# Sparse attention with mixture of experts: constants written in three pieces, and the placings of two batches at other units

## The chip, the core and the metric

The kernel runs on one core of one Trainium2 chip. The time is device time in microseconds (us) of one execution. It was measured three times before the change; a profile of one further execution gives the trace. The engines are PE (TensorE, matmuls), DVE (VectorE), ACT (ScalarE), POOL (GpSimd) and SP (which only issues DMAs here). Each engine works through its own list of instructions strictly in order, and waits at an instruction until all that it needs is there.

## What is computed

Chunk-selected causal attention over 4 batches of 8 heads with 768 positions and 64 columns, then a mixture of experts over the 3072 resulting tokens: a dense two-layer part for every token, and for each token one of 8 experts, chosen by the largest logit and weighted by its softmax value.

```python
# attention: the 6 best chunks of 32 keys by an upper bound, then causal softmax
ub = np.sum(np.maximum(q[:, :, :, None, :] * k_min[:, :, None, :, :], q[:, :, :, None, :] * k_max[:, :, None, :, :]), axis=-1)
top_chunks = np.argsort(ub, axis=-1)[..., -top_k:]
mask = sel & (pos[:, None] >= pos[None, :])
scores = np.where(mask, scores, -1000000000.0)
...
# mixture of experts on x = the attention output, a row per token
y_dense = np.maximum(x @ w1_dense, 0.0) @ w2_dense
expert_idx = np.argmax(x @ w_gate, axis=1)
for e in range(E):
    mask = expert_idx == e
    h = np.maximum(x[mask] @ w1[e], 0.0)
    y_moe[mask] = gate_w[mask, None] * (h @ w2[e])
return (y_dense + y_moe).astype(np.float32)
```

## The kernel before

**The attention** runs over 16 pairs of heads, four pairs to a batch; here pair 0 to pair 15. A pair has 11 units, 0 to 10. A unit computes a tile of up to 128x512 scores on PE (`scores`, L603), takes the exponential on ACT into `ex` (L607), and multiplies it with the values on PE (`av`, L622, into `op`). Scores are issued two units ahead of their `av`. In units 0, 5 and 6 the tile lies on the diagonal, and POOL masks `ex` (the select, L609) between ACT and the `av`. When a head's last `av` is done, DVE normalises it (`norm`, L631 and L633) into `xbig`, the batch's token rows. There are two `xbig`, so batch 2 writes the one that batch 0 used.

**Preparation for later pairs** runs beside this: SP loads k, q and v; POOL casts v of pair p+2 at unit 0 of pair p (L534) and k and q of pair p+3 at unit 7 (L527, L529); PE turns them round (L540, L560, L589); DVE reduces keys to chunk extremes `ks` (L545), multiplies them with a mask into `kb` (L548), copies halves of k (L552, L553), and finds the best chunks by MAX8 (L581) into flags `fl` (L583). PE needs `kb` for the bounds `ub` (L575). POOL also issues the casting loads of the weights: `wd` (L206, L208) and the experts' `we` (L213), one to three in a pair.

**A finished batch** is worked on during the next batch's 44 units, in slots that `batch_fills` keys by number; the slot of key n runs at unit n+1 of the batch. PE turns token rows round (L262), computes the gate (L270), the dense layers (L407, L423) and, at key 15, each token's row number in its expert's list (`ranks`, which ends in `slot` on DVE, L307). Then `place(t)`, for t from 0 to 5, has POOL scatter 128 token rows of `xbig` into `table` by an indirect DMA (L387). `place(0)` is preceded by a small copy of token numbers (L381). The placings stood at keys 18, 21, 24, 27, 30 and 33: units 8 of the batch's second pair, 0, 3, 6 and 9 of its third, and 1 of its fourth.

**The constants** that gate, ranks, placings and lists need are written by `route_consts`, all at once at unit 0 of pair 2, behind the value cast and the second `wd` load. It ends with a DMA on SP of an empty block, `zt`, into `table` (L194).

**The order** on each engine is set when the program is built: a helper schedules instructions by their dependences, and `tc.issue_after` pins an instruction behind another; `latest["pool"]` is the select issued last. The last batch's tail (from about 160 us) runs the experts over fetched rows of `table` and scatters their outputs from POOL.

Of the kernel before, what the change touches and what calls it, by code (L numbers as in the profile page):

```python
# [12 lines left out]
ALU = mybir.AluOpType  # L13
# [4 lines left out]
def kernel(  # L18
# [147 lines left out]
    nblk = const.tile([1, 1], mybir.dt.int32)  # L166
    xbig = [const.tile([128, NT, XW], HF, name=f"xbig{i}") for i in range(2)]

    def route_consts():
        for x2 in xbig:  # L170
            nc.gpsimd.memset(x2[:, :, Dm:XW], 0.0)
        nc.gpsimd.iota(iom8, pattern=[[0, NT], [1, E]], base=-E, channel_multiplier=0, allow_small_or_imprecise_dtypes=True)
        nc.gpsimd.memset(osum[:, 0], 0.0)
        nc.gpsimd.memset(eone, 1.0)
        nc.gpsimd.memset(used, 0.0)
        for i in range(EF):
            nc.gpsimd.memset(we_[:, :, i : i + 1], float(E**i))
        for i in range(RF):
            nc.gpsimd.memset(wr_[:, :, i : i + 1], float(256**i))
        for f in (EF, RF):  # L180
            for t in fields[f]:
                nc.gpsimd.memset(t, 0.0)
        nc.gpsimd.memset(ones, 1.0)
        nc.gpsimd.memset(low, 1.0)
        nc.gpsimd.affine_select(out=low, in_=low, compare_op=ALU.is_gt, fill=0.0,
                                base=0, pattern=[[1, 128]], channel_multiplier=-1)
        nc.gpsimd.iota(ebase[:, 0], pattern=[[CAP // 128, E]], base=0, channel_multiplier=0, allow_small_or_imprecise_dtypes=True)
        nc.gpsimd.iota(erow, pattern=[[CAP, E]], base=0, channel_multiplier=0, allow_small_or_imprecise_dtypes=True)
        nc.gpsimd.iota(iob, pattern=[[1, NBLK]], base=0, channel_multiplier=0, allow_small_or_imprecise_dtypes=True)
        for j in range(NJ):  # L190
            nc.gpsimd.iota(num[64 * j : 64 * j + 64, :, 0], pattern=[[128, NM]], base=j, channel_multiplier=2)
        nc.gpsimd.memset(zt, 0)
        nc.gpsimd.memset(zt[:, Dm + 2 : Dm + 4].bitcast(mybir.dt.int32), NONE)
        nc.sync.dma_start(out=table[EMPTY : EMPTY + 128], in_=zt)  # L194


    wd = const.tile([128, 2 * NK, 512], HF)
# [55 lines left out]
    def batch_fills(b):  # L253
# [197 lines left out]
        for n, f in zip((0, 2, 4, 6, 8, 10) + (12,), out_list):  # L451
            at.setdefault(n, []).append(f)
        at.setdefault(15, []).append(ranks)
        for t in range(NT):
            at.setdefault(18 + 3 * t, []).append(place(t))
        for n, f in zip((7, 8, 9, 10, 12, 13, 14, 15, 17, 18, 19, 20, 22, 23, 24, 25, 27, 28, 29, 30, 32, 33, 34, 35, 37, 38, 39, 40), dense):
            at.setdefault(n, []).append(f)
        return out_list, dense, ranks, [place(t) for t in range(NT)], at
# [56 lines left out]
    with (  # L515
# [234 lines left out]

        wq = [(e, w) for w in range(2) for e in range(E)]
        PER_PAIR = {**{p: 1 for p in range(4, 10)}, 10: 2, 11: 2, 12: 2, 13: 3}
        ahead_n = 2
        LAG = 1

# [11 lines left out]
        for i, (p, u) in enumerate(seq):  # L767
# [43 lines left out]
            if u == (6 if p == 0 else 0) and n2 is not None:  # L811
                with tc.issue_after(latest["pool"].ins):
                    cast_v(n2)
                load(p + 4, "v")
                if 1 <= p <= 2:
                    load_dense(st[n2]["cast"], p - 1)
                if p == 2:
                    with tc.issue_after(st[n2]["cast"].ins):
                        route_consts()
                for _ in range(PER_PAIR.get(p, 0)):  # L820
                    load_expert(*wq.pop(0), st[n2]["cast"])
            if u == 0 and p == NP - 2:
                while wq:
                    load_expert(*wq.pop(0), latest["pool"])
            if u == 7:
                with tc.issue_after(latest["pool"].ins):
                    cast_qk(p + 3)
                load(p + 5, "kq")
# [169 lines left out]
```

## Time and profile before

| | us |
|---|---|
| median of 3 runs (lowest, highest) | 246.07 (245.33, 246.31) |
| the profiled execution, its own time | 247.03 |
| its span in the trace | 245.3 |
| PE busy | 209.9 (86%) |
| DVE busy | 176.5 (72%) |
| ACT busy | 174.4 (71%) |
| POOL busy | 162.3 (66%) |

The span runs from the first to the last recorded instruction; 1.73 us of the profiled execution lie outside it. The share of an engine is an average over stages with different limits, so the stages have to be read one by one: a view by windows gives the busy time of each engine in a stretch, and the timeline of an engine gives its instructions in order of time, with the idle time before each and what ended it. A DMA row gives the time from issue to landing.

### The profile page before, as it was taken

Reading aid. Unit: us, or ns where it says so; the run is one execution under the profiler, and the core shown is the slowest. Engines: PE = TensorE matmul, PEld = TensorE weight load, DVE = VectorE, ACT = ScalarE, POOL = GpSimd, SP = SyncE. Lnnn points to the kernel's source line nnn. Section 1 sums busy time; section 2 is a strip of 40 time slices with the busy share of each in tenths; the row PEclk is TensorE's granted clock in tenths of the full one; section 3 lists DMA queues with packets and bytes.
Section 4 is the critical chain, followed back from the end, with each engine's and each line's share of the span. In section 5 each row is a group of like instructions: output and inputs, shape, how many; then the busy total and the mean of one; then the engine's idle time right before and its main releaser. Section 6 shows DMA issues by size and latency. Waiting matters only on the chain. (4 is left out here: it accounts for less than half of the span.)

```text
span 245.3 us, 7890 instructions
## 1 busy us (share of the span) xinstructions
PE 209.9 (86%) x2771; PEld 149.1 (61%) x2771; DVE 176.5 (72%) x561; ACT 174.4 (71%) x325; POOL 162.3 (66%) x213
## 2 busy tenths in 40 slices
PE   0688778798997989997999997989999989999950
PEld 0466455665665667754668665667566657777720
DVE  3889999999989789796978998677632225555410
ACT  4579797888787899596899986844566556666630
POOL 6458796677188767358878827620788748888881
PEclk9999999999999999999999999999999999999996
DMA  6999999999479899989999999356499999987785
GB/s 176 249 268 277 204 250 223 273 207 240 139 111 351 171 300 243 254 175 208 334 157 263 196 181 229 116 149 180 141 273 226 221 269 245 190 138 106 96 117 99
DMA packets 68279, 50.55 MB, mean 206 GB/s; under 512 B 29712, under 2 KB 61328, under 8 KB 68240
## 3 DMA queue, kind: packets, MB, share of 16 engines
q1 hardware_dynamic: 53008, 30.72, 46.7%
q0 software_dynamic: 15232, 19.32, 46.4%
q8 instruction: 23, 0.38, 0.6%
q14 instruction: 16, 0.13, 0.2%
HBM read 41.93 MB, written 18.23 MB: 245 GB/s over the span
## 5 line engine op out<-in xcount | busy, mean ns | idle before, releaser
L607 ACT ACTIVATE ex<-sp 128x512 f16<-128x512 f32 (+1 forms) x176 | 91.6, 606 | 10.3 <-PE sp L603 8.5
L603 PE MATMUL sp<-rT,kT 128*128 128x128 f16 (+3 forms) x384 | 64.2, 261 | 3.6 <-ACT ex L607 0.9
L609 POOL TENSOR_SCALAR_AFFINE_SELECT ex<-ex 128x512 f16<-128x512 f16 x48 | 32.5, 687 | 37.9 <-ACT ex L607 35.6
L897 POOL DMA_INDIRECT out_dram<-yo,xg x27 | 44.8, 1658 | 12.1 <-issue 4.9
L622 PE MATMUL op<-v,ex 128*128 128x65 f16 x672 | 46.0, 194 | 7.3 <-POOL ex L609 4.2
L622 PEld LDWEIGHTS <-ex 128*128 128x128 f16 x672 | 36.1, 98 | 23.1 <-POOL ex L609 8.1
L387 POOL DMA_INDIRECT table<-xbig,slot x24 | 24.4, 1015 | 17.8 <-issue 17.2
L860 DVE COPY exT<-tp 128x512 f16<-128x512 f16 x28 | 11.8, 423 | 33.1 <-PE tp L858 28.7
L603 PEld LDWEIGHTS <-kT 128*128 128x128 f16 x384 | 28.4, 98 | 7.5 <-issue 4.6
L867 PEld LDWEIGHTS <-w 128*128 128x128 f16 x432 | 26.4, 98 | 8.1 <-issue 2.4
L888 PE MATMUL yp<-we,ehT 128*128 x112 | 30.8, 378 | 0.5 <-ACT ys L428 0.2
L867 PE MATMUL hp<-exT,w 128*128 128x128 f16 x432 | 29.2, 219 | 0.8 <-issue 0.8
L407 PE MATMUL hp<-xT,wd 128*128 128x384 f16 x128 | 28.9, 325 | 0.6 <-DVE xT L263 0.6
L895 ACT ACTIVATE yo<-yp,xg 128x512 f32<-128x512 f32 x27 | 18.6, 687 | 14.0 <-PE yp L888 13.2
L545 DVE TENSOR_REDUCE ks<-kp 128x24 f16<-128x768 f16 x28 | 25.4, 946 | 3.6 <-ACT kp L542 3.3
L423 PE MATMUL yp<-wd,hT 128*128 128x512 f16 x96 | 25.9, 379 | 0.3
L870 ACT ACTIVATE ehT<-hp 128x512 f16<-128x512 f32 x28 | 16.7, 597 | 12.4 <-PE hp L867 9.1
L412 ACT ACTIVATE hT<-hp 128x384 f16<-128x384 f32 x30 | 14.9, 498 | 10.7 <-PE hp L407 10.1
L512 DVE COPY w<-we 128x2048 f16 x27 | 18.7, 694 | 0.2 <-DVE exT L860 0.2
L633 DVE TENSOR_TENSOR xbig<-op,rs 128x384 f16<-128x384 f32 x32 | 17.6, 550 | 0.3
L428 ACT COPY ys<-yp 128x512 f32<-128x512 f32 x21 | 12.7, 606 | 6.0 <-PE yp L423 5.9
L888 PEld LDWEIGHTS <-ehT 128*128 128x128 f16 x112 | 10.1, 97 | 10.2 <-issue 3.6
(158 smaller groups left out, 371.6 us busy)
## 6 DMA issues: line engine op xcount, KB each, us to landing
we<-in_moe_w_dram POOLq DMA_DIRECT2D x16, 512.0 KB, 7.6
kf<-in_k_dram SPq DMA_DIRECT2D x32, 192.0 KB, 4.0
qf<-in_q_dram SPq DMA_DIRECT2D x32, 192.0 KB, 4.5
vf<-in_v_dram SPq DMA_DIRECT2D x32, 192.0 KB, 4.8
out_dram<-ys SPq DMA_DIRECT2D x48, 128.0 KB, 5.3
xg<-table SPq DMA_DIRECT2D x27, 136.0 KB, 4.1
table<-zt SPq DMA_DIRECT2D x9, 136.0 KB, 2.4
wd<-in_moe_w_dense_dram POOLq DMA_DIRECT2D x2, 512.0 KB
```

The source lines that it names most:

```text
L387: sc = nc.gpsimd.indirect_dma_start(out=table, out_offset=bass.IndirectOffsetOnAxis(ap=keep["slot"][:, t : t + 1], axis=0), in_=xbig[b % 2 ...
L407: nc.tensor.matmul(hp, wd[:, ko, j * 128 : (j + 1) * 128], xT[:, ko, g * G * 128 : (g + 1) * G * 128], start=(ko == 0), stop=(ko == NK - 1))
L423: nc.tensor.matmul(yp, hold["h"][:, j, i * 128 : (i + 1) * 128], wd[:, NK + j], start=(j == 0), stop=(j == NK - 1))
L512: nc.vector.tensor_copy(w.rearrange("p j f -> p (j f)"), w1f[:, bass.ds(offs1[i], NK * 512)])
L545: nc.vector.tensor_reduce(out=ks[:, i], in_=kp.rearrange("d (c w) -> d c w", w=32), op=op, axis=mybir.AxisListType.X)
L603: last = nc.tensor.matmul(sp[:, o : o + w], kT[p % NB][g][:, kt * 128 : (kt + 1) * 128], rT[p % NB][g][:, a * 128 : z * 128], start=(o == ...
L607: scored.append((last, nc.scalar.activation(ex[:, 0:o], sp[:, 0:o], AF.Exp, scale=-0.125)))
L609: latest["pool"] = nc.gpsimd.affine_select(out=ex, in_=ex, compare_op=ALU.is_ge, fill=0.0, base=0, pattern=[[0, 4], [1, 2], [2, 64]], chan ...
L622: nc.tensor.matmul(s["op", g][:, t * (D + 1) : (t + 1) * (D + 1)], ex[:, o : o + 128], v16[p % NB][:, g, kt, :], start=first, stop=(last_o ...
L867: nc.tensor.matmul(hp[:, j], s["w1"][:, ko, j * 128 : (j + 1) * 128], s["xT"][:, ko], start=(ko == 0), stop=(ko == NK - 1), skip_group_che ...
L888: nc.tensor.matmul(yp, s["hT"][:, j], w2f[:, bass.ds(offs[i] + j * 512, 512)], start=(j == 0), stop=(j == NK - 1))
L897: sc = nc.gpsimd.indirect_dma_start(out=out, out_offset=to, in_=o, in_offset=None, bounds_check=N - 1, oob_is_err=False, compute_op=ALU.by ...
```

## The change

`route_consts` takes a part number. Part 0 holds the tails of both `xbig`, `iom8`, the first `osum`, `ones` and `low`; part 1 `ebase`, `num`, the empty block `zt` and its DMA; part 2 all the small ones of the lists (`eone`, `used`, the weights, the fields, `erow`, `iob`). They are issued at unit 5 of pairs 3, 4 and 5, behind the select issued last (that of unit 6), where all stood at unit 0 of pair 2. For batches 0 and 1 the placings move to keys 25, 26, 31, 36, 37 and 42: units 4, 5 and 10 of the batch's third pair and the same of its fourth. Batch 2 keeps its keys.

```diff
-    def route_consts():
+    def route_consts(part):
+        if part == 0:
             for x2 in xbig:
                 nc.gpsimd.memset(x2[:, :, Dm:XW], 0.0)
...
+        elif part == 1:
...
-        for t in range(NT):
-            at.setdefault(18 + 3 * t, []).append(place(t))
+        for t, n in enumerate((25, 26, 31, 36, 37, 42) if b < B - 2 else range(18, 36, 3)):
+            at.setdefault(n, []).append(place(t))
...
+        CONSTS = (3, 4, 5)
...
-                if p == 2:
-                    with tc.issue_after(st[n2]["cast"].ins):
-                        route_consts()
...
+            if u == 5 and p in CONSTS:
+                with tc.issue_after(latest["pool"].ins):
+                    route_consts(CONSTS.index(p))
```

On POOL in pair 2, before: the value cast, the load of `wd`, the constants (30 instructions, cut here), then the selects of units 5 and 6 and the cast of k.

```order
L534 CAST v_1_119<-vf 128x12x64
L208 DMA wd<-in_moe_w_dense_dram 128x4x512
L171 MEMSET xbig_171 128x6x32
...
L193 MEMSET zt 128x1
L609 AFFINE_SELECT ex<-ex 128x512 x2
L527 CAST k_902<-kf 128x768
```

The same place after, and on to pair 3 (lines are numbered three higher from `route_consts` on):

```order
L537 CAST v_1_119<-vf 128x12x64
L211 DMA wd<-in_moe_w_dense_dram 128x4x512
L612 AFFINE_SELECT ex<-ex 128x512 x2
L530 CAST k_871<-kf 128x768
L532 CAST q_873<-qf 128x768
L612 AFFINE_SELECT ex<-ex 128x512
L537 CAST v_2_120<-vf 128x12x64
L612 AFFINE_SELECT ex<-ex 128x512 x2
L172 MEMSET xbig_171 128x6x32
...
L176 MEMSET low 128x128
L530 CAST k_1069<-kf 128x768
```

The selects of pair 2 now follow the load of `wd` at once, and a first piece of the constants stands between the selects of pair 3 and its cast of k.

On POOL in pairs 6 and 7, before, batch 0's placings stand round the selects of units 5 and 6 of pair 6, and ahead of the value cast of pair 7:

```order
L387 DMA table<-xbig_171,slot 25728x544 x2
L609 AFFINE_SELECT ex<-ex 128x512
L387 DMA table<-xbig_171,slot 25728x544
L609 AFFINE_SELECT ex<-ex 128x512
L387 DMA table<-xbig_171,slot 25728x544
L527 CAST k_1832<-kf 128x768
L529 CAST q_1834<-qf 128x768
L609 AFFINE_SELECT ex<-ex 128x512
L387 DMA table<-xbig_171,slot 25728x544 x2
L534 CAST v_0_118<-vf 128x12x64
L213 DMA we_175<-in_moe_w_dram 128x4x512
L609 AFFINE_SELECT ex<-ex 128x512 x2
```

After, from the selects of pair 7's units 5 and 6 into pair 8, whose unit 0 select is the first single one:

```order
L612 AFFINE_SELECT ex<-ex 128x512 x2
L390 DMA table<-xbig_171,slot 25728x544 x2
L530 CAST k_2058<-kf 128x768
L532 CAST q_2060<-qf 128x768
L612 AFFINE_SELECT ex<-ex 128x512
L390 DMA table<-xbig_171,slot 25728x544
L537 CAST v_1_119<-vf 128x12x64
L216 DMA we_175<-in_moe_w_dram 128x4x512
L612 AFFINE_SELECT ex<-ex 128x512 x2
```

The fourth and fifth placing now stand behind pair 7's selects, and the sixth in pair 8, ahead of its value cast, its expert load and its selects of units 5 and 6. In pair 6 the first two stand between the casts of k and of q, behind both selects; batch 1 has the same pattern in pairs 10, 11 and 12.

On DVE in pair 8, the normalisation that first writes batch 2's rows into batch 0's `xbig`, with the semaphores that it waits for; six of them are those of batch 0's placings, before and after:

```order
L631 RECIPROCAL rs<-op 128x6 [waits PE_49]
L633 TENSOR_TENSOR xbig_171<-op,rs 128x6x64 [waits DMASW3_49,DMASW2_49,DMASW6_49,DMASW1_49,DMASW7_49,DMASW0_49,DVE_49]
L545 TENSOR_REDUCE ks<-kp 128x24 [waits Activation_49]
...
L564 TENSOR_SCALAR rT_0_114<-pq 128x768 [waits Activation_49]
L548 TENSOR_TENSOR kb<-ks,hmask 128x96 [waits DVE_49]
```

```order
L634 RECIPROCAL rs<-op 128x6 [waits PE_49]
L636 TENSOR_TENSOR xbig_171<-op,rs 128x6x64 [waits DMASW4_49,DMASW3_49,DMASW6_49,DMASW2_49,DMASW7_49,DMASW0_49,DVE_49]
L548 TENSOR_REDUCE ks<-kp 128x24 [waits Activation_49]
...
L567 TENSOR_SCALAR rT_0_114<-pq 128x768 [waits Activation_49]
L551 TENSOR_TENSOR kb<-ks,hmask 128x96 [waits DVE_49]
```

Its place on DVE has not moved, while the last of the placings that it waits for has moved from pair 7 to pair 8.

## Rows read from the trace of the kernel before

**Rows 1.** The view by windows of 20 us over all engines: start and end, length, then busy time and number of instructions of PE, its weight loads, DVE, ACT and POOL, the granted PE clock as a share of 2.4 GHz, the DMA share and GB/s.

```profile
20.00:40.00 20.00, 15.95 (x251) 11.27 (x249) 19.43 (x54) 16.83 (x33) 16.88 (x50) 1.00 1.15 241
...
100.00:120.00 20.00, 17.93 (x261) 12.62 (x257) 16.61 (x58) 15.68 (x33) 11.84 (x16) 1.00 1.03 235
```

**Rows 2.** POOL's timeline in pair 2, at and behind the constants: start, busy us, what, and the idle time before it with what ended it.

```profile
32.78 0.48 POOL L171 MEMSET xbig<- 128x192 f16 x2
...
33.41 0.17 POOL L174 MEMSET eone<- 1x8 f32 x1
...
34.00 0.19 POOL L183 MEMSET ones<- 128x128 f16 x1
...
34.29 0.13 POOL L187 IOTA ebase<- 128x8 f16 x1
34.38 0.13 POOL L188 IOTA erow<- 1x8 f32 x1
...
34.60 0.36 POOL L191 IOTA num<- 64x24 int32 x2
...
35.52 0.29 POOL L185 TENSOR_SCALAR_AFFINE_SELECT low<-low 128x128 f16<-128x128 f16 x1
...
35.82 1.27 POOL L609 TENSOR_SCALAR_AFFINE_SELECT ex<-ex 128x512 f16<-128x512 f16 x2
...
37.81 0.82 POOL L529 CAST q<-qf 128x768 f16<-128x768 f32 x1
```

**Rows 3.** ACT's timeline in pair 2: the six exponentials of units 4 to 9.

```profile
32.59 3.03 ACT L607 ACTIVATE ex<-sp 128x384 f16<-128x384 f32 x6
```

**Rows 4.** DVE's timeline in pairs 1 to 3; the reductions L545 come once in a pair.

```profile
27.06 1.80 DVE L545 TENSOR_REDUCE ks<-kp 128x24 f16<-128x768 f16 x2
...
32.80 0.68 DVE L553 COPY kT<-kp 64x768 f16<-64x768 f16 x1
...
35.39 1.80 DVE L545 TENSOR_REDUCE ks<-kp 128x24 f16<-128x768 f16 x2
...
37.81 0.88 DVE L548 TENSOR_TENSOR kb<-ks,hmask 128x96 f16<-128x96 f16 x1
...
43.81 1.80 DVE L545 TENSOR_REDUCE ks<-kp 128x24 f16<-128x768 f16 x2
...
46.23 0.21 DVE L548 TENSOR_TENSOR kb<-ks,hmask 128x96 f16<-128x96 f16 x1
```

**Rows 5.** PE's timeline: the two waits in pair 2, the wait in pair 6, two products of pair 8 (units 5 and 6), the wait in pair 10 and the products of unit 5 in pair 12.

```profile
36.53 0.30 PE L622 MATMUL op<-v,ex 128*128 128x65 f16 x4 [0.62 <-POOL ex L609]
37.15 0.30 PE L622 MATMUL op<-v,ex 128*128 128x65 f16 x4 [0.32 <-POOL ex L609]
...
77.84 0.21 PE L575 MATMUL ub<-kb,qp 128*128 128x48 f16 x2 [1.25 <-DVE kb L548]
...
91.14 0.30 PE L622 MATMUL op<-v,ex 128*128 128x65 f16 x4
...
112.69 0.30 PE L622 MATMUL op<-v,ex 128*128 128x65 f16 x4 [1.62 <-POOL ex L609]
...
132.82 0.32 PE L622 MATMUL op<-v,ex 128*128 128x65 f16 x5
```

**Rows 6.** POOL's timeline in pairs 6 to 8: the cast and the select about `kb` in pair 6, the select of pair 7's unit 6, and the start of pair 8.

```profile
76.28 0.83 POOL L529 CAST q<-qf 128x768 f16<-128x768 f32 x1
77.05 0.67 POOL L609 TENSOR_SCALAR_AFFINE_SELECT ex<-ex 128x512 f16<-128x512 f16 x1
...
83.27 0.67 POOL L609 TENSOR_SCALAR_AFFINE_SELECT ex<-ex 128x512 f16<-128x512 f16 x1 [0.84 <-ACT ex L607]
...
88.00 0.74 POOL L609 TENSOR_SCALAR_AFFINE_SELECT ex<-ex 128x512 f16<-128x512 f16 x1 [2.53 <-ACT ex L607]
...
90.42 1.28 POOL L609 TENSOR_SCALAR_AFFINE_SELECT ex<-ex 128x512 f16<-128x512 f16 x2 [0.17 <-ACT ex L607]
```

**Rows 7.** DVE's timeline: `kb` in pair 6, a key copy and the first normalisation of pair 8, and a key copy in pair 11.

```profile
76.39 1.40 DVE L548 TENSOR_TENSOR kb<-ks,hmask 128x96 f16<-128x96 f16 x1
...
87.05 0.31 DVE L552 COPY kT<-kp 64x768 f16<-64x768 f16 x1
...
92.60 0.56 DVE L633 TENSOR_TENSOR xbig<-op,rs 128x384 f16<-128x384 f32 x1
...
118.79 0.36 DVE L553 COPY kT<-kp 64x768 f16<-64x768 f16 x1
```

**Rows 8.** POOL's timeline in pairs 10 to 12: batch 1's placings, and the selects of pair 12's units 5 and 6.

```profile
109.60 1.04 POOL L387 DMA_INDIRECT table<-xbig,slot  x1 [1.64 <-issue]
110.94 1.01 POOL L387 DMA_INDIRECT table<-xbig,slot  x1 [0.31 <-issue]
111.96 0.67 POOL L609 TENSOR_SCALAR_AFFINE_SELECT ex<-ex 128x512 f16<-128x512 f16 x1
...
118.73 0.98 POOL L387 DMA_INDIRECT table<-xbig,slot  x1 [0.17 <-issue]
...
130.99 1.30 POOL L609 TENSOR_SCALAR_AFFINE_SELECT ex<-ex 128x512 f16<-128x512 f16 x2
```

**Rows 9.** The DMA view of two windows of some 1 us, each with one placing: its queue, the number of issues, and the us from issue to landing. The first is batch 0's first placing, the second batch 1's fifth.

```profile
table<-xbig,slot POOLq DMA_INDIRECT x1, 6.5
...
table<-xbig,slot POOLq DMA_INDIRECT x1, 5.1
```

More of the change, by code (lines that the diff above doesn't have):

```diff
@@ L167 @@
     xbig = [const.tile([128, NT, XW], HF, name=f"xbig{i}") for i in range(2)]
-    def route_consts():
[L170 to L194, printed above, removed]
@@ new lines, in route_consts @@
+    def route_consts(part):
+        if part == 0:
+            for x2 in xbig:
+                nc.gpsimd.memset(x2[:, :, Dm:XW], 0.0)
+            nc.gpsimd.iota(iom8, pattern=[[0, NT], [1, E]], base=-E, channel_multiplier=0, allow_small_or_imprecise_dtypes=True)
+            nc.gpsimd.memset(osum[:, 0], 0.0)
+            nc.gpsimd.memset(ones, 1.0)
+            nc.gpsimd.memset(low, 1.0)
+            nc.gpsimd.affine_select(out=low, in_=low, compare_op=ALU.is_gt, fill=0.0,
+                                    base=0, pattern=[[1, 128]], channel_multiplier=-1)
+        elif part == 1:
+            nc.gpsimd.iota(ebase[:, 0], pattern=[[CAP // 128, E]], base=0, channel_multiplier=0, allow_small_or_imprecise_dtypes=True)
+            for j in range(NJ):
+                nc.gpsimd.iota(num[64 * j : 64 * j + 64, :, 0], pattern=[[128, NM]], base=j, channel_multiplier=2)
+            nc.gpsimd.memset(zt, 0)
+            nc.gpsimd.memset(zt[:, Dm + 2 : Dm + 4].bitcast(mybir.dt.int32), NONE)
+            nc.sync.dma_start(out=table[EMPTY : EMPTY + 128], in_=zt)
+        else:
+            nc.gpsimd.memset(eone, 1.0)
+            nc.gpsimd.memset(used, 0.0)
+            for i in range(EF):
+                nc.gpsimd.memset(we_[:, :, i : i + 1], float(E**i))
+            for i in range(RF):
+                nc.gpsimd.memset(wr_[:, :, i : i + 1], float(256**i))
+            for f in (EF, RF):
+                for t in fields[f]:
+                    nc.gpsimd.memset(t, 0.0)
+            nc.gpsimd.iota(erow, pattern=[[CAP, E]], base=0, channel_multiplier=0, allow_small_or_imprecise_dtypes=True)
+            nc.gpsimd.iota(iob, pattern=[[1, NBLK]], base=0, channel_multiplier=0, allow_small_or_imprecise_dtypes=True)
```

## Prediction

> **What bounds the kernel now.** I read the windows first, because the shares over the whole span mix stages. In 20 to 40 us (pairs 1 to 3, no batch work yet) DVE is busy 19.43 of 20 us and PE only 15.95: there DVE sets the pace. From pair 4 on PE also carries a finished batch, and in 100 to 120 us it is busy 17.93 of 20 us, DVE 16.61, POOL 11.84 [rows 1]. POOL is nowhere full, so the time it spends on constants or placings costs nothing by itself. It costs what stands behind it in POOL's order and is waited for: the selects, for which PE's `av` waits, and through the port that POOL shares with DVE some copies. So I then looked for PE's waits in the stretches of the change and asked what ended them [rows 5]. There are four above 0.3 us: two selects in pair 2 (0.62 and 0.32), `kb` in pair 6 (1.25), and a select in pair 10 (1.62). Together they are 3.8 us, which is about all that this change can take away.
>
> **Constants leave pair 2.** They hold POOL from 32.78 to 35.82, 3.04 us, and the selects of units 5 and 6 stand behind them [rows 2]. ACT did the six exponentials of units 4 to 9 in 32.59 to 35.62, some 0.5 each, so unit 5's was ready at about 33.6 [rows 3]: the select is 2.2 us late, and PE waits 0.62 + 0.32 = 0.94 us [rows 5]. But DVE sets the pace here, so the gain is what DVE gets back. Its reduction comes at 27.06, 35.39 and 43.81, distances of 8.33 and 8.42 us [rows 4]. Two DVE instructions in them are stretched while POOL works: the key copy L553 at 32.80 takes 0.68 beside the constants' memset, against 0.36 for the same copy elsewhere [rows 7], 0.32 us; and `kb` at 37.81 takes 0.88 beside the cast of q (also 37.81), against 0.21 in pair 3 [rows 2, 4], 0.67 us. With the constants gone that cast ends some 2 us earlier and is out of the way. DVE gains up to 0.32 + 0.67 = 0.99 us.
>
> **The pieces come back in pairs 3, 4 and 5**, between the selects and the cast of k. From the starts [rows 2]: part 0 is (33.41 - 32.78) + (34.29 - 34.00) + (35.82 - 35.52) = 1.22 us; part 1 is (34.38 - 34.29) + (35.52 - 34.60) = 1.01; part 2 is (34.00 - 33.41) + (34.60 - 34.38) = 0.81; in sum 3.04. No select is queued directly behind them, but the casts of k and q are, and then unit 0's select of the next pair, 2 us or more of POOL work later. The casts are needed a pair later, so 1 us is covered. In pair 3 the moved cast of q may now meet `kb` (46.23, unhindered at 0.21 before [rows 4]): 0 to 0.67 lost, I take 0.3. In pairs 4 and 5 I take nothing, and the DMA of `zt` on SP, now ahead of the k loads of a pair five later, also nothing: those loads have more than a pair of slack. **Sum for the constants: -0.7 us**, between -1.0 and 0.
>
> **Placings, pair 10 (batch 1).** The first waits 1.64 us on POOL for `slot` and starts at 109.60; two of them then hold POOL to 111.95, and unit 5's select comes at 111.96 [rows 8]. PE waits 1.62 us for it [rows 5]. After the change both selects stand ahead of the placings. Next late is then PE's own order and the flags on DVE, up to 0.3 us. **-1.5**, between -1.64 and -1.0.
>
> **Placings, pair 6 (batch 0).** PE's 1.25 us is for `kb`, which takes 1.40 from 76.39 [rows 5, 7] and ends as POOL ends its cast of q (76.28 to 77.11) and the select behind it (to 77.72) [rows 6]: two POOL instructions back to back held it. After the change the cast of q stands behind two placings of about 1.0 with gaps of 0.3 [rows 8], while the selects come some 1.5 us earlier: these nearly cancel, and whether `kb` asks just before the cast or just after it starts can't be read. **-0.6**, half of it, between -1.25 and 0.
>
> The fitting rule is in the Trainium skill, SBUF — State Buffer, "SBUF: two separate sides": DVE and GpSimd share a port pair that the first to start keeps for its whole instruction. For casts and memsets the rows above agree. By the rule placings should also hold DVE's copies back, and then pair 6 would keep its wait. But the copy L553 at 118.79 took 0.36, no longer than normal, within a placing that ran 118.73 to 119.71 [rows 7, 8]; I go by that row in the sum and keep the other as a rival.
>
> **What is late next: pairs 7 to 8.** The select of pair 7's unit 6 starts at 83.27 and ends at 83.94 on ACT's account [rows 6]. Behind it now stand two placings, 0.17 + 0.98 + 0.30 + 1.0, then the casts of k and q at about 0.8 each, to 88.0: just when unit 0's exponential of pair 8 lets its select start (88.00) [rows 6, 8]. So that select is not late, but the casts now run beside DVE's key copies at 87.05 (0.31 before [rows 7]), which may each be held by part of an instruction. Then comes the sixth placing, 1.15 with its gap, ahead of the value cast, the expert load and the selects of units 5 and 6. Those selects start at 90.42 before [rows 6], 0.17 of which was idle, so they come about 1.0 late. PE takes unit 5's product at 91.14, right as its select ends [rows 5, 6]: no slack, but the new order puts further scores ahead of it. Then DVE's normalisation at 92.60 must wait until the sixth placing has landed: started at 88.0 + 0.74 + 0.15 = 88.9, and landing 5.1 us after issue as batch 1's fifth did [rows 9], that is 94.0, 1.4 us late for DVE, of which `kb` and the rest have slack for most. **+0.8**, between 0 and +2.0.
>
> **Pairs 11 to 12** have the same order. The selects of units 5 and 6 (130.99 [rows 8]) come about 1.1 late, but PE takes those products only at 132.82 [rows 5], so most is covered. **+0.4**, between 0 and +1.2. Batch 2's placings, the last batch and the tail are unchanged and start earlier or later with the attention.
>
> **Sum.** -0.7 - 1.5 - 0.6 + 0.8 + 0.4 = -1.6 us. On the profiled execution: 245.3 - 1.6 = 243.7 of span, and 247.03 - 1.6 = 245.4 of its time. That execution lies 0.96 us above the median of the runs, so for the median I take 246.07 - 1.6 = 244.5.
>
> **Rivals.**
> (a) The waits only change hands. A PE that is early in pair 10 finds DVE or ACT late, and DVE in pairs 2 to 3 loses at other casts what it gained: pair 10 is worth 0.8, the constants 0.3, pair 6 nothing, pairs 8 and 12 cost 0.8: 246.07 - 0.3 = 245.8. For it: DVE has under 0.6 us idle in 20 to 40 us [rows 1]; against it: in pair 10 DVE itself stood idle with PE.
> (b) Slower: the sixth placing lands late. If it takes 6.5 us like batch 0's first [rows 9], which was issued behind an expert load, it lands at 95.4, and DVE stands still 2.8 us in pair 8. With 0.8 for the held selects, 0.4 in pair 12, and gains of only 2.2 without pair 6, that is 246.07 + 1.8 = 247.9. It decides from a landing of about 92.60 - 88.9 = 3.7 us upward; against it: the placing is no longer issued just behind an expert load.
> (c) Placings hold the port as casts do: pair 6 keeps 1.25, and each key copy of pairs 8 and 12 that meets a placing waits up to 1.0, two copies each, half of them met: the sum becomes -0.7 - 1.5 + 0.8 + 0.4 + 2.0 = +1.0, 247.1. That is the case which the Trainium skill's rule above would give.
>
> **Chances.** The forecast 0.5, (a) 0.31, (b) 0.13, (c) 0.06. A measurement of this kernel tells about 0.5%, 1.2 us, from no change: faster means under 244.8, slower over 247.3. Of the forecast's 0.5, its own bounds leave some 0.12 inside 1.2 us; (a) gives 0.08 to faster, (c) is half slower. Faster 0.46, same 0.39, slower 0.15. All terms at their best give -3.9 us (242.2), at their worst +2.2 (248.3). Leaving out a tenth at each end the range is 242.6 to 247.4; faster and same hold most of it.
>
> **What would show it.** Right: in pair 2 the selects start at about 33.6, and the DVE reductions of pairs 2 and 3 come about 1 us earlier; in pair 10 PE has no wait above 0.4 us for a select; in pair 8 PE waits under 1 us. Wrong: `kb` in pairs 3 or 6 above 1 us; a normalisation in pair 8 that ends an idle time of DVE above 1 us with a DMA named as its releaser (b); a key copy over 0.8 us with nothing but a placing beside it (c). Attention's end against before tells the whole, as the tail should not change its length; a change of the tail by over 0.5 us would make the sum wrong in a place that I have not priced.

## The result and the profile after

The change made the kernel slower: 247.61 us median (15 runs) against 245.84 (15 runs), a ratio of 1.0074, 95% interval 1.0051 to 1.0098. Ratios, here and below, leave out runs that took over 1.5% longer than the shortest of the same kernel. The profiled execution after has a span of 247.7 us against 245.3. So 1.6 us were forecast to go, and 1.8 came by the medians, 2.4 between the two profiled executions.

Where they came is read from the starts of the normalisations (`norm` on DVE, two in a pair, one for each head; L633 before, L636 after), since each closes a stretch of attention:

| normalisation | before | after | shift | what lies between |
|---|---|---|---|---|
| pair 1, first head | 32.23 | 32.10 | -0.13 | start, ahead of the constants |
| pair 2, second head | 43.34 | 42.48 | -0.86 | constants: -0.73 |
| pair 6, first | 73.73 | 72.87 | -0.86 | |
| pair 6, second | 80.56 | 79.92 | -0.64 | pair 6: +0.22 |
| pair 7, first | 87.28 | 88.39 | +1.11 | pair 7: +1.75 |
| pair 7, second | 89.65 | 91.82 | +2.17 | +1.06 |
| pair 8, second | 98.41 | 100.71 | +2.30 | pair 8: +0.13 |
| pair 9, second | 109.46 | 111.77 | +2.31 | |
| pair 10, second | 120.59 | 121.30 | +0.71 | pair 10: -1.60 |
| pair 11, first | 127.31 | 129.00 | +1.69 | pair 11: +0.98 |
| pair 12, second | 140.24 | 142.55 | +2.31 | pairs 11, 12: +0.62 |
| pair 15, second | 163.45 | 165.89 | +2.44 | |

The tail keeps its length: 81.9 us from the last normalisation before, 81.8 after. The constants and pair 10 did what was forecast. On POOL the selects of units 5 and 6 of pairs 2 and 10 follow their exponentials at once (before, [rows 2, 8]):

```profile
33.58 1.28 POOL L612 TENSOR_SCALAR_AFFINE_SELECT ex<-ex 128x512 f16<-128x512 f16 x2 [0.91 <-ACT ex L610]
...
111.18 1.47 POOL L612 TENSOR_SCALAR_AFFINE_SELECT ex<-ex 128x512 f16<-128x512 f16 x2 [0.92 <-ACT ex L610]
```

On DVE in pairs 2 and 3 the copy and the key mask `kb` have their plain lengths, and the reductions come 8.0 us apart, not 8.4 as in [rows 4]:

```profile
26.93 1.80 DVE L548 TENSOR_REDUCE ks<-kp 128x24 f16<-128x768 f16 x2
...
32.67 0.36 DVE L556 COPY kT<-kp 64x768 f16<-64x768 f16 x1
34.94 1.80 DVE L548 TENSOR_REDUCE ks<-kp 128x24 f16<-128x768 f16 x2
37.36 0.21 DVE L551 TENSOR_TENSOR kb<-ks,hmask 128x96 f16<-128x96 f16 x1
...
42.94 1.80 DVE L548 TENSOR_REDUCE ks<-kp 128x24 f16<-128x768 f16 x2
```

The loss sits in pairs 6 to 8, and once more in 11 and 12. PE's timeline of after, the three longest waits of pairs 6 to 8, each with what ended it:

```profile
77.20 0.21 PE L578 MATMUL ub<-kb,qp 128*128 128x48 f16 x2 [1.46 <-DVE kb L551]
...
87.47 0.21 PE L578 MATMUL ub<-kb,qp 128*128 128x48 f16 x2 [1.00 <-DVE kb L551]
...
91.96 0.51 PE L592 MATMUL ps<-ident,fl 128*128 128x128 f16 x6 [1.49 <-DVE fl L586]
```

PE waits for DVE, not for POOL. And DVE is late because single instructions of it are long. Before, the mask of pair 7 and the second key copy behind it had their plain lengths:

```profile
86.12 0.20 DVE L548 TENSOR_TENSOR kb<-ks,hmask 128x96 f16<-128x96 f16 x1
...
87.86 0.36 DVE L553 COPY kT<-kp 64x768 f16<-64x768 f16 x1
```

After, with the mask of pair 6 as the first line and the normalisation of pair 8 as the last:

```profile
75.53 1.61 DVE L551 TENSOR_TENSOR kb<-ks,hmask 128x96 f16<-128x96 f16 x1
...
85.48 1.94 DVE L551 TENSOR_TENSOR kb<-ks,hmask 128x96 f16<-128x96 f16 x1
...
88.96 1.43 DVE L556 COPY kT<-kp 64x768 f16<-64x768 f16 x1
...
94.45 0.56 DVE L636 TENSOR_TENSOR xbig<-op,rs 128x384 f16<-128x384 f32 x1
```

POOL beside them:

```profile
74.61 1.01 POOL L390 DMA_INDIRECT table<-xbig,slot  x1 [0.30 <-issue]
75.62 0.84 POOL L532 CAST q<-qf 128x768 f16<-128x768 f32 x1
76.41 0.67 POOL L612 TENSOR_SCALAR_AFFINE_SELECT ex<-ex 128x512 f16<-128x512 f16 x1
...
84.77 0.97 POOL L390 DMA_INDIRECT table<-xbig,slot  x1 [0.30 <-issue]
85.75 0.83 POOL L530 CAST k<-kf 128x768 f16<-128x768 f32 x1
86.52 0.83 POOL L532 CAST q<-qf 128x768 f16<-128x768 f32 x1
...
88.19 1.13 POOL L390 DMA_INDIRECT table<-xbig,slot  x1 [0.17 <-issue]
89.33 0.84 POOL L537 CAST v<-vf 128x768 f16<-128x768 f32 x1
```

The three long instructions were each asked late inside a placing (0.92, 0.71 and 0.77 us after its start) and ended only when what stood directly behind that placing was done: at 77.14 (select to 77.08), 87.42 (cast of q to 87.35) and 90.39 (cast of v to 90.17). Over the whole span the last 14 of the 16 `kb`, 15 first and 15 second key copies take 4.9, 7.6 and 6.0 us before and 7.1, 8.4 and 7.7 after, 4.7 us more. The normalisation at 94.45 has no idle time before it, 6.3 us after the sixth placing's start (88.19): rival (b), that placing landing late, is not seen here. In pair 11 it is the same picture on DVE, with a placing from 126.18 and the casts of k and q from 127.21 to 128.86:

```profile
126.86 0.56 DVE L551 TENSOR_TENSOR kb<-ks,hmask 128x96 f16<-128x96 f16 x1
...
128.15 0.93 DVE L555 COPY kT<-kp 64x768 f16<-64x768 f16 x1
```

**Theory 1 (port):** DVE's copies and masks from SBUF wait for a memory port that POOL holds, and a placing right ahead of a cast makes that hold longer. **Rivals:** POOL's own order is what is late; or pair 10's gain is only the delay of pair 8 made up again, and the loss is something else.

### The profile page after: what moved, and what is told of

Read it like the earlier page. It is cut to its first block, busy times and chain, and to the rows that moved or that the text cites. A ratio compares the mean times of both kernels' runs of the same rounds, so it can differ in the third digit from the quotient of the medians.

```text
span 247.7 us, 7887 instructions
## 1 busy us (share of the span) xinstructions
PE 209.6 (85%) x2771; PEld 149.2 (60%) x2771; DVE 181.2 (73%) x561; ACT 174.4 (70%) x325; POOL 162.6 (66%) x213
## 5 line engine op out<-in xcount | busy, mean ns | idle before, releaser
L901 POOL DMA_INDIRECT out_dram<-yo,xg x27 | 44.3, 1640 | 12.3 <-issue 5.8
L636 DVE TENSOR_TENSOR xbig<-op,rs 128x384 f16<-128x384 f32 x32 | 17.6, 549 | 0.3
```

What stands on the lines that cost most here:

```text
L901: sc = nc.gpsimd.indirect_dma_start(out=out, out_offset=to, in_=o, in_offset=None, bounds_check=N - 1, oob_is_err=False, compute_op=ALU.by ...
```

## Experiments

The kernels ran in four groups, each on another chip beside runs of the kernel before: 1 to 4; 6 to 8 and the first of 12 to 14; 5, 9, 10 and the second of 12 to 14; 11 and the third. The kernel before took 246.9 us (median) in the first group and 255.2 to 255.4 in the others. Most of that difference lies behind the attention: kernel 7 starts its last normalisation at 165.92 of a span of 253.1, kernel 1 at 162.99 of 244.2. So ratios to before are compared, and starts of normalisations within a group or lengths within one trace. Pair 6 isn't the same on every chip: kernels 6 and 7 and the first and third of 12 to 14 take 21.6 us from pair 4's first normalisation to pair 6's first, 19.96 in the first group, and their `kb` of pair 6 is not held (0.20). There is no trace of the kernel before from those chips, so their ratios can hold something of pair 6 too.

**1. The constants alone.** All placings at their old keys.

```diff
-        for t, n in enumerate((25, 26, 31, 36, 37, 42) if b < B - 2 else range(18, 36, 3)):
+        for t, n in enumerate((range(18, 36, 3), range(18, 36, 3), range(18, 36, 3))[min(b, 2)]):
```

> The constants in three pieces alone; all placings at every third unit from 18, as in the kernel before. Theory 1 (the loss comes from the placings of the first two batches, behind which DVE's copies and the key mask wait for the memory port that POOL holds) and its rivals agree here: in the changed kernel POOL's select of pair 7 stood 0.64 us earlier and those of pairs 3 to 6 some 0.85 us earlier, so 245.84 - 0.7 = 245.1 us, with pairs 7 to 15 all shifted by about -0.8. If the constants themselves cost something later (pair 5's piece), 245.8 or more.

Measured 0.9946 (0.992 to 0.9971). The constants are a gain by themselves, of 0.7 us in the forecast and 0.7 to 2.0 here. The traces have 0.75 us: from pair 1's first normalisation to pair 2's second are 10.37 us, 11.12 before.

**2 and 3. One batch's placings at a time**, with the constants in pieces.

```diff
+        for t, n in enumerate(((25, 26, 31, 36, 37, 42), range(18, 36, 3), range(18, 36, 3))[min(b, 2)]):
...
+        for t, n in enumerate((range(18, 36, 3), (25, 26, 31, 36, 37, 42), range(18, 36, 3))[min(b, 2)]):
```

> Constants in three pieces, and the placings of batch 0 alone at the new units; batch 1's stay at every third from 18. Theory 1: the 3.2 us lost in pairs 6 to 9 are there and pair 10's 1.6 us are not won, since its placings are the old ones: 245.84 - 0.86 + 0.22 + 3.0 = 248.2 us. Rival (the gain of pair 10 was no gain of the moved placings but the delay of pair 8 being made up in a stage where POOL was the late one): pair 10 gives 1.6 us back here as well, 246.6 us.

> Constants in three pieces, and the placings of batch 1 alone at the new units; batch 0's stay at every third from 18. Theory 1: pair 10 gives 1.6 us and pairs 12 and 13 take 1.8 us: 245.84 - 0.8 - 1.6 + 1.8 = 245.3 us. Rival (pair 10's gain was the delay of pair 8 being made up): no gain in pair 10, only the loss of pairs 12 and 13: 246.8 us.

Measured 1.005 (1.0017 to 1.0084) and 0.9945 (0.991 to 0.9979). The first lies between the two expectations, the traces decide. Against the constants alone the second head's normalisation of pair 6 stands at -0.59 with batch 0's keys, pair 8's at +2.35, pair 9's at +2.34 and the first of pair 10 still at +2.34 (112.86 and 115.20): 2.9 us are lost in pairs 7 and 8, and pair 10 gives nothing back. With batch 1's keys pairs 2 to 9 stand at -0.1, the first head of pair 10 at -1.84 (111.02) and pair 12's second at -0.11 (139.79): pair 10's 1.74 us belong to batch 1's own first two placings, and pairs 11 and 12 take them back. The rival of a delay made up is out. Here batch 0's move is pure loss, batch 1's a gain that is lost again.

**4. What holds what.** A kernel with nothing but POOL's work beside streams of one DVE operation.

```diff
+    for dve_op, n in ((op_kb, 40), (op_copy, 24), (op_psum, 16), (op_red, 40)):
+        section([put] * 4, dve_op, n)
+        section([cast] * 4, dve_op, n // 2)
+        section([put, cast, put, cast], dve_op, n)
```

> None of the computation is done: a kernel that only sets POOL's work beside a stream of one kind of VectorE operation and writes zeros. Twelve stretches: four placings, four casts, or placing and cast in turn on POOL, each beside a stream of (a) the key mask's multiply of two SBUF inputs, 128x96 f16, (b) the key copy, 64x768 f16 from SBUF, (c) the same copy from PSUM, (d) a reduce of one SBUF input. Theory 1: (a) and (b) are held to the end of a cast, as the 0.8 us casts held them in the kernel, and by a placing from about its middle on, up to 0.4 us for one that is asked then; where a cast follows on the placing, to the cast's end; (c) and (d) keep their usual length beside all. Rival (a placing holds nothing, and what was late in pairs 7 and 8 was late for POOL's order alone): (a) and (b) have their usual 0.21 and 0.36 us through a placing's whole length, and only casts hold them.

Its DVE timeline shows 24 key copies as one row: beside four placings (one behind the other), then beside placing and cast in turn.

```profile
25.24 7.37 DVE L102 COPY kt<-kp 64x768 f16<-64x768 f16 x24
...
39.27 9.42 DVE L102 COPY kt<-kp 64x768 f16<-64x768 f16 x24
```

Beside placings alone a copy takes 0.31 us on average (7.37 / 24). Read one by one, the copies start 0.27 apart where POOL is idle, and each of the four placings makes about 0.2 us of it longer (a copy of 0.56 at 26.37, of 0.54 at 27.66 and 28.93): a placing itself holds a copy, but by half of the 0.4 that theory 1 had. With casts between, the stream is 2.05 us longer still. In that stretch one copy, at 40.13, took 1.73: it was asked 0.31 into a placing (39.82) and ended at 41.86, behind the cast (40.80 to 41.64). Copies from PSUM (0.47 each) and reduces (0.16) keep their length in all three settings. It also goes the other way: beside a stream of masks one placing took 3.67 us.

**5. The same, one operation at a time** (run with the third group). One placing, behind it nothing, a cast or a second placing, and one DVE operation at six offsets.

```diff
+    for dve_op in (op_kb, op_copy):
+        for follow in ([], [cast], [put]):
+            for n in range(4, 10):
+                single(follow, dve_op, n)
```

> None of the computation is done: the kernel sets one placing on POOL and, at six offsets into it (0.1 to 0.9 us), one VectorE operation, and writes zeros. Behind the placing stands nothing that is ready, or a cast, or a second placing. Theory 1 (port), as the first probe left it: with nothing or a placing behind, the key copy (64x768 f16) keeps 0.31 to 0.36 us at every offset and the key mask (two SBUF inputs) is held, up to 0.4 us, to the placing's end if it is asked in the later half; with a cast ready behind, both are held from their asking inside the placing to the cast's end, 1 to 1.7 us. Rival: the hold is the cast's alone, so both run before the cast starts if they are asked more than their own length ahead of it.

Three settings on POOL: a placing with nothing ready behind it, one with a cast, one with a second placing (the first three rows for `kb`, the others for the copy).

```profile
6.86 0.98 POOL L89 DMA_INDIRECT table<-x,slot  x1
...
19.75 0.98 POOL L89 DMA_INDIRECT table<-x,slot  x1
20.73 0.83 POOL L97 CAST v<-vf 128x768 f16<-128x768 f32 x1
...
66.56 0.98 POOL L89 DMA_INDIRECT table<-x,slot  x1
67.55 0.83 POOL L97 CAST v<-vf 128x768 f16<-128x768 f32 x1
...
84.57 0.98 POOL L89 DMA_INDIRECT table<-x,slot  x1
```

The DVE operation asked 0.47 to 0.48 us into each of these four placings:

```profile
7.33 0.20 DVE L100 TENSOR_TENSOR kb<-ks,hm 128x96 f16<-128x96 f16 x1
...
20.22 1.42 DVE L100 TENSOR_TENSOR kb<-ks,hm 128x96 f16<-128x96 f16 x1
...
67.03 1.57 DVE L103 COPY kt<-kp 64x768 f16<-64x768 f16 x1
...
85.05 0.34 DVE L103 COPY kt<-kp 64x768 f16<-64x768 f16 x1
```

| asked into the placing, us | 0.15 | 0.31 | 0.47 | 0.63 | 0.79 | 0.95 |
|---|---|---|---|---|---|---|
| `kb`, nothing or a placing behind | 0.19, 0.20 | 0.20 | 0.20 | 0.20 | 0.20 | 0.20 |
| `kb`, a cast behind | 0.20 | 0.20 | 1.42 | 1.26 | 1.10 | 0.94 |
| key copy, nothing or a placing behind | 0.34 | 0.34 | 0.34 | 0.51 | 0.34, 0.35 | 0.34 |
| key copy, a cast behind | 0.34 | 0.34 | 1.57 | 1.41 | 1.25 | 1.09 |

A placing holds little (0.17 us of a copy at one offset). But a cast that is ready behind it holds what is asked 0.47 us into the placing, some 0.5 us before the start that the trace records for the cast, and to the cast's end; in experiment 4 it held a copy asked 0.31 in, here none. Behind a placing a cast of 0.83 holds DVE 1.4 us. Most of what I had put down to the placing is the cast.

**6. The fourth and fifth of the six placings alone**, right ahead of the casts of pair 7.

```diff
+        for t, n in enumerate(((18, 21, 24, 27, 36, 37), range(18, 36, 3), range(18, 36, 3))[min(b, 2)]):
```

> Constants in three pieces; of the placings only batch 0's fourth and fifth (of six, counted from one: the fifth and sixth of the row, t = 4 and 5) are moved, from 30 and 33 to 36 and 37, which puts them on POOL right ahead of the casts of pair 7. From the constants alone (244.5 us on the scale of 245.84 before). Theory 1 (port): the key mask of that preparation is asked while the second of the two runs and is held over it and over both casts, 1.7 us; the copies behind it then fall into the next cast, 0.4 to 0.6 us more: 246.4 us (246.0 to 246.9). Rival (the lateness is POOL's own): POOL stood idle 2.5 us ahead of pair 8's select, the two placings take 2.3 us of it, so nothing is late: 244.5 us.

DVE in pair 7 of this kernel:

```profile
84.91 1.92 DVE L551 TENSOR_TENSOR kb<-ks,hmask 128x96 f16<-128x96 f16 x1
87.57 0.31 DVE L555 COPY kT<-kp 64x768 f16<-64x768 f16 x1
...
88.38 0.66 DVE L556 COPY kT<-kp 64x768 f16<-64x768 f16 x1
```

Measured 0.9994 (0.9963 to 1.0026), 0.9946 being the constants alone. Against the next kernel, which ran beside it, the second head of pair 6 stands at -0.85 (79.36 and 80.21) and the first of pair 7 at +0.87 (87.80 and 86.93): 1.72 us lost in one place, as theory 1 had it (1.7). In pairs 7 and 8 PE has no wait above 0.25 us for a select of POOL. For this loss the rival of POOL's own order is out.

**7. The last placing alone**, behind pair 8's first select.

```diff
+        for t, n in enumerate(((18, 21, 24, 27, 30, 42), range(18, 36, 3), range(18, 36, 3))[min(b, 2)]):
```

> Constants in three pieces; of the placings only batch 0's last (t = 5) is moved, from 33 to 42, behind the first select of pair 8 and ahead of that pair's value cast. Theory 1 (port): the second key copy was held by this placing and the cast behind it in the changed kernel only because the key mask before it had come late; here it is asked before the placing starts, so it keeps 0.36 us and the time is that of the constants alone, 244.5 us (244.2 to 244.9). Rival (the sixth placing by itself costs what pair 8 lost, through the cast and the selects behind it): 245.5 us.

Measured 1.0009 (0.9974 to 1.0043): theory 1 missed, while the rival's 245.5 (0.9986 of 245.84) lies within the interval. The copy kept 0.36 us (87.50), as theory 1 said, but DVE's timeline has something else:

```profile
93.28 0.56 DVE L636 TENSOR_TENSOR xbig<-op,rs 128x384 f16<-128x384 f32 x1 [0.93 <-DMA table<-xbig,slot]
```

The placing started at 88.55, and the normalisation that overwrites its rows stood still for its landing, 4.7 us later. That is rival (b) of the prediction. In the changed kernel the same normalisation came 6.3 us after the placing, since pair 8 was already late by the port. The landing is half of what is lost: from pair 6's second normalisation to pair 8's second are 19.65 us, 17.85 before. Pair 8's own mask and key copies, now later, stand beside its casts and take 0.54, 0.78 and 0.72 us (95.94, 97.42, 98.22), 0.20, 0.58 and 0.36 before.

**8. The key mask off the port**, with all placings as in the changed kernel. By experiment 4 reduces are not held.

```diff
-                                        axis=mybir.AxisListType.X)
-            s["kb"] = kb = ahead.tile([128, 2, 2, NC], HF, name="kb")
-            nc.vector.tensor_tensor(kb, ks.unsqueeze(2).to_broadcast([128, 2, 2, NC]), hmask, ALU.mult)
+                                        axis=mybir.AxisListType.X, negate=i == 1)
+            s["kb"] = kb = kbz[p % 2]
+            for g, h in ((0, 64), (1, 0)):
+                nc.vector.tensor_reduce(out=kb[h : h + 64, :, g], in_=ks[h : h + 64].unsqueeze(3), op=ALU.max,
+                                        axis=mybir.AxisListType.X)
```

> The changed kernel with all its placings, but the key mask is no longer a multiply of two SBUF inputs: the second reduce negates, and two small reduces copy the halves into tiles that are zero elsewhere. In the probe reduces kept their length beside placings and casts. Theory 1 (port): the 1.6 and 1.9 us masks of pairs 6 and 7 shrink to about 0.3, PE's waits for them (1.5 and 1.0 us) and most of what followed in pair 8 go, for some 0.15 us more DVE work a pair: 247.6 - 1.5 - 2.4 + 0.4 = 244.1 us (243.3 to 245.2). Rival (POOL's own lateness): nothing of it changes, 247.6 to 248.1 us.

Measured 1.0012 (0.9976 to 1.0049): a smaller gain than expected. DVE in pairs 7 and 8 (lines are numbered six higher):

```profile
85.36 0.41 DVE L556 TENSOR_REDUCE kbz<-ks 64x48 f16<-64x48 f16 x2
...
92.71 0.56 DVE L642 TENSOR_TENSOR xbig<-op,rs 128x384 f16<-128x384 f32 x1 [0.68 <-DMA table<-xbig,slot]
```

The 1.94 us became 0.41. From pair 6's second normalisation to pair 7's first are 6.60 us (80.20 to 86.80), against 6.72 before and 8.47 in the changed kernel: pair 7's loss is gone with the hold. Then the landing shows again, 0.68 us. And the two reduces cost where nothing held the mask: from pair 4's first normalisation to pair 6's first are 20.57 us, 19.96 before. (To pair 5's second they are 17.61 and 15.86, but there a MAX8 of 0.87 us stands ahead of the normalisation, and behind it before.)

**9. The same mask with the old placings.**

> Constants in three pieces, all placings as in the kernel before (every third unit from 18), and the key mask by two small reduces. The constants alone took 0.9946 of before. Theory 1 (port): pair 6's mask, 1.4 us in the kernel before [held over a cast and a select], shrinks to 0.3 and PE's wait of 1.2 us for it goes: 0.990 (0.987 to 0.993). Rival (the mask is late for its inputs): 0.994 to 0.997.

Measured 1.0032 (0.9995 to 1.0069), missed. Pair 4's first to pair 6's first normalisation take 20.94 us, 0.98 more than before. PE waits for DVE there, by the view of waits from 52 to 75 us (0.6 us in the kernel with the constants alone):

```profile
PE hp L414 <- DVE xT L270: 1.0, 1, 1.0
```

That is more than what comes back in pair 6 (6.07 us between its two normalisations, 6.83 before), and from pair 6's second to pair 12's second another 1.6 us are lost. I had priced it at 0.15 us a pair as if DVE had slack. Which DVE instruction costs what in the later pairs was not tried.

**10. The casts ahead of the fourth and fifth placing.** The same work on POOL ahead of the next select, in the other order.

```diff
-        for t, n in enumerate((25, 26, 31, 36, 37, 42) if b < B - 2 else range(18, 36, 3)):
+        for t, n in enumerate(((25, 26, 31, 40, 40, 42), (25, 26, 31, 40, 40, 42), range(18, 36, 3))[min(b, 2)]):
```

> The changed kernel, but the fourth and fifth of the six moved placings (t = 3 and 4, key 36 and 37) stand at 40, which puts them right behind the pair's two casts instead of right ahead of them. POOL has the same work ahead of the next pair's select. Theory 1 (port): the casts are done when the key mask is asked, which then waits at most for the rest of one placing (0.7 us in place of 1.7), in pair 7 as in pair 11: 1.0 to 1.5 us less in pairs 7 and 8 and 0.5 to 0.9 us less in pairs 11 and 12, so 0.998 of before (0.996 to 1.001) where the changed kernel took 1.007. Rival (POOL's amount of work ahead of the select is what is late): 1.007 as before.

DVE in pairs 7 and 8:

```profile
85.19 0.20 DVE L551 TENSOR_TENSOR kb<-ks,hmask 128x96 f16<-128x96 f16 x1
...
86.12 0.31 DVE L555 COPY kT<-kp 64x768 f16<-64x768 f16 x1
...
93.42 0.56 DVE L636 TENSOR_TENSOR xbig<-op,rs 128x384 f16<-128x384 f32 x1 [1.46 <-DMA table<-xbig,slot]
```

Measured 1.0041 (1.0001 to 1.008), between the expectations; the interval holds the rival's 1.007 too, so the trace decides. The mask was asked 0.49 us into a placing with another placing behind it, and took 0.20, as experiment 5 shows. From pair 6's second to pair 7's first normalisation are 6.72 us, as before. The hold is gone from pair 11 too (`kb` 0.20 at 125.39). What is left in pair 8 is the landing, 1.46 us. But pairs 11 and 12 stay as long: from pair 10's second normalisation to pair 12's second are 21.08 us, 21.25 in the changed kernel and 19.65 before. Pair 12's mask stands beside its value cast (from 135.18), its second copy beside loads of `we`:

```profile
135.24 0.83 DVE L551 TENSOR_TENSOR kb<-ks,hmask 128x96 f16<-128x96 f16 x1
...
137.59 0.77 DVE L556 COPY kT<-kp 64x768 f16<-64x768 f16 x1
```

**11. The last placing earlier as well.**

```diff
-        for t, n in enumerate(((25, 26, 31, 40, 40, 42), (25, 26, 31, 40, 40, 42), range(18, 36, 3))[min(b, 2)]):
+        for t, n in enumerate(((25, 26, 31, 32, 40, 40), (25, 26, 31, 32, 40, 40), range(18, 36, 3))[min(b, 2)]):
```

> The changed kernel with batch 0's and 1's placings at (25, 26, 31, 32, 40, 40): against the run with the casts ahead of the fourth and fifth placing, the last placing is issued ahead of pair 8's (pair 12's) first select and no longer behind it. Theory 2 (the port's hold hid a second cost: the last placing lands after the norm of pair 8 wants to write the rows that it reads, which idled VectorE 1.5 us in that run and 0.9 us in the run of the sixth alone): that idle time is 0 to 0.3 us, pair 8 gives 1.0 to 1.5 us back: 0.994 to 0.998 of before where that run took 1.004. Rival (port alone; the 1.5 us stood beside other waits): 1.002 to 1.005.

Measured 0.9967 (0.9934 to 1.0001), the time that theory 2 had. DVE:

```profile
84.31 0.20 DVE L551 TENSOR_TENSOR kb<-ks,hmask 128x96 f16<-128x96 f16 x1
...
91.58 0.56 DVE L636 TENSOR_TENSOR xbig<-op,rs 128x384 f16<-128x384 f32 x1 [0.38 <-DMA table<-xbig,slot]
94.24 0.72 DVE L551 TENSOR_TENSOR kb<-ks,hmask 128x96 f16<-128x96 f16 x1
```

The idle time fell from 1.46 to 0.38 us. Pair 8's own mask now falls into its value cast (94.08) and loses 0.5: moving one piece shifts the phase of the next collision. By pair 8's second normalisation nothing is won: from pair 6's second are 19.92 us, 19.63 in experiment 10. So the lower time is not shown to come from the landing. And POOL's order costs now, in pair 11, where the two last placings (to 127.67) stand right ahead of a select, on PE:

```profile
128.44 0.30 PE L625 MATMUL op<-v,ex 128*128 128x65 f16 x4 [1.01 <-POOL ex L612]
```

Two key copies beside these placings were held with no cast near, the first before another placing, the second (asked at 0.33 into its placing) before that select:

```profile
125.95 0.54 DVE L555 COPY kT<-kp 64x768 f16<-64x768 f16 x1
...
126.97 0.88 DVE L556 COPY kT<-kp 64x768 f16<-64x768 f16 x1
```

**12 to 14. Other places.** Batch 0 at (18, 21, 24, 31, 32, 40) and batch 1 at (25, 26, 29, 31, 32, 40); the same with the mask by reduces; and batch 1's keys of these with batch 0's old ones.

> Constants in three pieces, batch 0's placings at (18, 21, 24, 31, 32, 40), batch 1's at (25, 26, 29, 31, 32, 40): none stands ahead of a pair's key and query casts except the ones that POOL does between them, and pair 10's first two stay behind that pair's selects. Theory 1 (port): constants -1.3 by the run of them alone, pair 10 -1.7 as in the run of batch 1, pairs 11 and 12 without their 1.5 us of loss, pair 6's mask 0 to 1.0 us sooner since the casts come 1.2 us sooner: 242.3 us (241.5 to 243.2). Rival (POOL's own lateness): two placings between pair 7's select and its value cast delay that pair's next selects by 1.2 us, which takes the gain of pair 6 or pair 10 back: 244 us or more.

> Constants in three pieces, the placings at (18, 21, 24, 31, 32, 40) in batch 0 and (25, 26, 29, 31, 32, 40) in batch 1, and the key mask by two small reduces as well. The same placings with the multiply took 0.9888 of before, and its profile still held three masks (0.56 us in pair 8, 0.4 to 0.7 us of copies behind it). Theory 1 (port): the mask out of the port's way gives some 0.8 us more in pair 8 and costs some 0.15 us of DVE a pair, so 0.984 to 0.988 of before. Rival (the mask was not what held pair 8): 0.988 to 0.991, the reduces being longer.

> Constants in three pieces, batch 0's placings as in the kernel before, batch 1's at (25, 26, 29, 31, 32, 40), none with a key or query cast ready right behind it but the second. Against the constants alone (0.9946): pair 10's 1.7 us are won and pairs 11 and 12 take back 0.3 to 1.0 us, where the changed units took 1.7 us: 0.989 to 0.993 of before. Rival (pairs 11 and 12 lose for the order on POOL, not the port): 0.995 or more.

Measured 0.9888 (0.9844 to 0.9933), 0.9989 (0.9946 to 1.0032) and 0.9855 (0.9789 to 0.9922). The first is faster than the kernel before and, by its ratio, than the changed one, on four of its six runs. For the third this is not shown: its ratio rests on three of seven runs, and the median of all seven is 255.20 against 255.36. Why the second, on another chip, did worse than the first is open: in both traces the last normalisation starts at 163.93. In the first, pair 8 lost 1.0 us to a mask beside the value cast (0.77 at 94.47) and to copies. In the third pair 10 gives 1.74 us and pairs 11 to 12 take back 0.96 (second normalisation of pair 12 at 138.83, -1.07 against the constants alone where pair 9 stood at -0.29); in pair 13 that execution then loses 4.0 us, a value cast waiting 4.03 us for its load (138.32), so its trace does not tell what the whole is worth.

## Why the prediction was wrong

**Constants, -0.7:** right; -0.86 us by pair 6 in the trace, 0.13 of which stood there before the constants begin. The 0.3 taken off for pair 3 was not lost: `kb` there took 0.25 (45.37).

**Pair 10, -1.5:** right; -1.60, and experiment 3 shows that it is batch 1's first two placings behind the selects.

**Pair 6, -0.6:** wrong, +0.22. The step held that the cast of q would come away from `kb` or meet it half the time. The placing ahead of that cast gave `kb` (75.53) no gap: it was held over the rest of the placing, the cast and the select, 1.61 us. That is one of the prediction's own signs of being wrong.

**Pairs 7 to 8, +0.8 with 0 to +2.0:** this is the step that failed, at +2.94. It priced key copies "held by part of an instruction", and left out `kb`, which stands ahead of them. The sum went by one row, the copy at 118.79 that took 0.36 inside a placing [rows 7, 8]. That row is true and was read too far, for two reasons. Behind that placing stood another placing, where experiment 5 has a hold of 0.17 us at most; the changed order put casts there. And the copy was asked only 0.06 us into the placing. In the trace after, the same copy (119.50) is asked as early, has a cast behind the placing, and keeps its length too:

```profile
119.44 0.98 POOL L390 DMA_INDIRECT table<-xbig,slot  x1 [0.17 <-issue]
120.43 0.85 POOL L537 CAST v<-vf 128x768 f16<-128x768 f32 x1
...
119.50 0.36 DVE L556 COPY kT<-kp 64x768 f16<-64x768 f16 x1
```

Experiments 6, 8 and 10 show the cause in place for pair 7: 1.72 us come with the two placings ahead of the casts, and go when the mask leaves the port or the casts come first. From pair 6's second normalisation to pair 7's first are 8.44 to 8.47 us in the three kernels with this order and a mask on the port (the changed one, 2 and 6), and 6.60 to 7.10 in all others. The next 1.06 us are the key copy at 88.96, behind the sixth placing and the value cast. Pair 8 stays long in each kernel with the sixth placing moved, for the landing and later casts: from pair 6's second to pair 8's second are 20.79 us in the changed kernel, 18.47, 19.63 and 19.92 in experiments 8, 10 and 11, and 17.85 before.

**Pairs 11 to 12, +0.4 with 0 to +1.2:** too small, +1.60. I had looked for late selects; in pair 11 it was again `kb` and a copy behind placing and casts, and these go in experiment 10. But pairs 11 and 12 still lose 1.42 us there, with pair 12's mask and copy held and no placing near them: what sets that part stays open.

**Rival (b)** gave 247.9 and its mechanism is real: experiments 7 and 10 have it at 0.9 and 1.5 us of idle time, and experiment 11 leaves 0.4. In the changed kernel it stayed hidden, as pair 8 was late already. **Rival (c)**, chance 0.06, gave 247.1 against 247.6 and came nearest in kind: DVE's port users held near the placings. Its mechanism was mostly not right, since a placing alone held about 0.2 us in the probes, not up to 1.0. The row that I dismissed it by could not tell the two apart. **Rival (a)** didn't happen in pairs 2 and 10, whose gains are whole. For pairs 11 and 12 it is not out: every kernel with batch 1's placings moved takes 20.3 to 21.25 us from pair 10's second normalisation to pair 12's second, 19.65 before, whether `kb` of pair 11 is held or not.

Two things stay open. Beside a placing the hold is not always what experiment 5 would have: the mask at 126.86 in pair 11 ran as the placing ended (127.42), though a cast was next, and in experiment 11 copies were held up to 0.5 us with none. And the landing was waited for 4.7 us after the last placing's start in experiment 7, 5.4 in experiment 10 (87.98 to 93.42) and 6.4 in experiment 11 (85.14 to 91.58), all on other chips than the one of the changed kernel: a start 2.8 us earlier gave a landing 1.8 us earlier, and what sets its length was not tried.

## What to carry to other kernels

When POOL instructions are moved, look at what becomes neighbours on POOL, not only at what moves: a placing ahead of a cast made a hold of 0.8 us one of 1.4, and two casts one of 1.9. A row that shows an operation unhindered counts only for its own neighbourhood and its own moment, and needs a second row with the neighbour and the offset that the change will bring. And a loss can hide a second one: after each cure read again which wait ends last, before the cure is called too weak.

## What the runs showed of the hardware

That the casts' hold begins so early was not expected. The Trainium skill, SBUF — State Buffer, "SBUF: two separate sides", has the shared port pair go to whichever of the two starts first, for its whole instruction; the mask and the copy held to the casts' ends agree (87.42 behind 87.35, 41.86 behind 41.64). The hold began some 0.5 us before the cast's recorded start, though (0.47 us into a placing of 0.98), while POOL was recorded as still at the placing. The Trainium skill, Perfetto Trace Analysis, "GPSIMD Engine Instruction", says that the recorded start is that of the first read and not of the instruction; this would fit, and no run here shows it.

The same port works against POOL: a stream of 40 masks stretched a placing from 0.98 to 3.67 us. Reduces (0.16 us each) and copies from PSUM (0.47) kept their length in all three settings of experiment 4.
